# A new order of work in the first four blocks of a conv and squared-ReLU kernel, with one weight half swapped by TensorE

## Chip, cores, metric

One core of one Trainium2 chip. The metric is the device time of one execution in microseconds (us). The mean clock granted to TensorE in one execution lies between 0.995 and 1.000 of full speed. The span of a profile is the same execution as the profiler saw it; it is 1.6 to 2.3 us shorter than the device time.

## The reference, cut to what matters

```python
# 8 sequences of 4096 rows, 192 columns; 8 heads of 24 columns; 7 taps
w = softmax(weight_gen, axis=-1)                   # (8, 4096, 8, 7)
x_unf[b, s, k] = x_pad[b, s + k]                   # 6 rows of zeros ahead
out = einsum('bshk,bskhg->bshg', w, x_unf)         # each row has its own 7 taps
h = maximum(out.reshape(32768, 192) @ w_in, 0)     # w_in 192 x 2048
return (h * h) @ w_out                             # w_out 2048 x 192
```

## The kernel before

All 32768 rows are cut into 64 sub-blocks of 512 and these into blocks: two blocks of one sub-block, then 31 of two. A block goes through four stages, on four engines:

- Softmax (ScalarE exp, VectorE sum, reciprocal, product), in parts of 8 to 32 rows per partition. Part 0 (1024 rows) feeds blocks 0 and 1, part 1 (sub-blocks 2 and 3) block 2, part 2 block 3, part 3 block 4, and so on.
- Weight rows are moved by DMA, multiplied on VectorE into a band matrix (`st_bands`), and TensorE does the convolution as band matmuls (`st_conv`, "C" below). ScalarE copies the result y out of PSUM.
- The first matmul in 8 or 16 units (`st_unit`, "u"): TensorE into one of three PSUM tiles, ScalarE relu into t, VectorE square into g.
- The second matmul in half quarters ("M"): a quarter is 256 rows, summed over all of g into one bank (blocks 0 and 1) or two; then ScalarE copies the bank out, VectorE adds the second bank.

```python
ps_h = ...bufs=3     # three tiles of two banks: h, y of the conv, and before also the spins
ps_o = ...bufs=1     # banks o0 and o1

orders = {0: "uuuuuCuuu", 1: "MuMuuuMuuuMCu", 2: "MuuuuMuuuuMuuuuuuuMCu"}
steady = "MuMuuu" * 3 + "MuuuMCu"
...                                        # softmax and bands: a table by block and unit
at(0, 4, "exp", s1, 0, s1.rh)
at(0, 5, "soft", s1, 0, s1.rh)

spin(42)                                   # matmuls on zeros, to bring TensorE's clock up
band_mask()
s0.load(nc.sync)
load_w_in(w_st[0], 0, nc.sync); x_load_f32(0); load_w_in(w_st[1], 1, nc.sync)
s0.exp(...); s0.total(...); s0.recip(...); s0.scale(...)
nc.scalar.copy(out=w_i[:, 0, 0], in_=w_st[0])
wr_load_sbuf(0, [s0], (0, 2, 1, 4, 3), (nc.sync, nc.gpsimd))   # weight rows of block 0
wr_load_sbuf(1, [s0], range(NT), (nc.gpsimd,))
cross_w_in(0)                              # SBUF to SBUF: halves of 64 partitions exchanged
x_cast(0, nc.scalar.copy)
x_load_f32(1)
nc.scalar.copy(out=w_i[:, 1, 0], in_=w_st[1])
cross_w_in(1)
s1.load(nc.sync)                           # the same queue: softmax weights of part 1
... # bands and conv of block 0, then
nc.gpsimd.memset(x_st[1][:, 0:1], 0.0)     # waits for the cast of x of sub-block 1
for q in range(4): load_w_out(q, 4)
s2.load(nc.gpsimd)
nc.gpsimd.memset(v_big, 0.0)
... # block 0, in it the rows of part 1 moved (also on GpSimd's queue); then
x_load(2); x_load(3)
```

Each half of `w_in` is needed on both halves of the partitions, so it is swapped across them; `cross_w_in` does that with two transfers of 192 KB each.

The softmax here doesn't subtract the row's maximum and nothing guards it: scores larger than these inputs give would overflow.

## Time and profile before

| | before |
|---|---|
| device time, median of 4 | 751.65 us (751.18 to 752.27) |
| span of the profiled run | 749.2 us |
| TensorE / ScalarE / VectorE busy | 739.0 / 623.0 / 621.8 us |
| TensorE idle | 10.2 us |
| first unit of block 0 starts | 15.47 us |
| conv of blocks 2, 3, 4, 5 starts | 36.65, 55.50, 78.41, 100.96 us |

Only the first 100 us are of interest: from there on every block takes 22.5 us with TensorE never idle, but for a few of 22.7 to 23.2. In a timeline line the columns are start, length, engine, line of the program, what was done, how many of them; in brackets the idle time before and what ended it. PE is TensorE, ACT ScalarE, DVE VectorE, POOL GpSimd, SP SyncE. The conv starts are the mile posts of this document: the conv of block n+1 stands at the end of block n.

### The profile page before, as it was taken

The page shows a single profiled execution, that of the slowest core. Times are in us where ns is not written, and L with a number is a line of the kernel's source. Part 1 is how long each engine was busy: PE and PEld are TensorE (multiplying, and loading weights), DVE is VectorE, ACT ScalarE, POOL GpSimd, SP SyncE. Part 2 cuts the span into 40 slices and gives each one's busy share as a digit, 9 for nine tenths or more (in the row PEclk, how much of TensorE's full clock was granted, in tenths as well). Part 3 has the DMA queues.
Part 4 walks back from the last instruction along what each step waited for, and adds up shares of the span by engine and source line. Part 5 has one row for each costly group of instructions (what it writes and reads, how often), then busy time and mean ns, then how long its engine had stood idle before and what let it go on. Part 6 is the DMA issues. An engine that isn't in the chain of part 4 may idle for free.

```text
span 749.2 us, 33282 instructions
## 1 busy us (share of the span) xinstructions
PE 739.0 (99%) x15106; PEld 559.8 (75%) x15106; DVE 621.8 (83%) x1001; ACT 623.0 (83%) x753; POOL 87.9 (12%) x127
## 2 busy tenths in 40 slices
PE   8899999999999999999999999999999999999998
PEld 4658777777887777777877777777778777777787
DVE  5889998998789888887888888898888987677853
ACT  4898888888888888888888888888888888888883
POOL 3522220001101000011000110001100011001000
PEclk9999999999999999999999999999999999999999
DMA  8846444446453344543245442365441354441312
GB/s 231 129 74 135 79 68 109 101 78 138 93 109 69 74 77 80 131 86 65 46 80 139 86 80 49 55 138 108 59 79 47 57 109 80 59 75 50 50 45 65
DMA packets 122329, 65.20 MB, mean 87 GB/s; under 512 B 83881, under 2 KB 118668, under 8 KB 121676
## 3 DMA queue, kind: packets, MB, share of 16 engines
q1 hardware_dynamic: 77868, 46.05, 22.4%
q0 software_dynamic: 44176, 16.93, 20.6%
q8 instruction: 118, 1.93, 1.1%
q14 instruction: 23, 0.19, 0.1%
q10 hardware_dynamic: 144, 0.10, 0.0%
HBM read 48.61 MB, written 28.70 MB: 103 GB/s over the span
## 4 chain that ended last, share of the span: by engine, by line
PE 88%; DVE 5%; DMA 3%; ACT 1%; issue 1%; SPq 0%; POOL 0%; DVEq 0%; ACTq 0%
PE o L453 42%; PE h L419 40%; PE yp L394 6%; DVE g L431 2%; DVE bd L326 1%; DMA xt<-in_x_dram 1%; ACT t L428 1%; DMA x_st<-in_x_dram 1%; DMA vd<-v_big 1%; DVE v_first L217 1%; DVE ssum L202 0%; DVE rcp L209 0%; DMA wg<-in_weight_gen_dram 0%; DVE o_sb L469 0%; POOL wr L308 0%
## 5 line engine op out<-in xcount | busy, mean ns | idle before, releaser
L428 ACT ACTIVATE t<-h 128x1024 f16<-128x1024 f32 x512 | 497.1, 1027 | 66.9 <-PE h L419 66.6
L431 DVE TENSOR_TENSOR g<-t 128x1024 f16<-128x1024 f16 x512 | 334.5, 687 | 101.9 <-ACT t L428 99.1
L453 PEld LDWEIGHTS <-g 64*128 64x128 f16 (+1 forms) x8032 | 353.0, 94 | 55.7 <-issue 5.0
L453 PE MATMUL o<-w_o,g 64*128 64x192 f16 (+1 forms) x8032 | 386.1, 243 | 1.7 <-DMA w_o<-in_moe_w_out_dram 0.7
L419 PE MATMUL h<-y,w_i 64*128 64x512 f16 (+1 forms) x3168 | 379.8, 370 | 2.1 <-ACT t L428 0.9
L419 PEld LDWEIGHTS <-w_i 64*128 64x128 f16 x3168 | 165.5, 94 | 114.7 <-issue 5.0
L326 DVE TENSOR_TENSOR bd<-wr,mask 128x4160 f16<-128x4160 f16 (+3 forms) x89 | 149.4, 1702 | 4.6 <-DMA wr<-v_first 4.6
L278 POOL DMA_DIRECT2D xt<-in_x_dram x62 | 51.3, 832 | 446.1 <-PE yp L394 422.8
L467 ACT COPY o_sb<-o 128x384 f32<-128x384 f32 x129 | 62.3, 483 | 33.2 <-PE o L453 33.2
L469 DVE TENSOR_TENSOR o_sb<-o,o_sb 128x384 f32<-128x384 f32 x123 | 68.2, 554 | 8.0 <-ACT o_sb L467 5.6
L405 ACT CAST y<-yp 128x1024 f16<-128x1024 f32 (+1 forms) x64 | 48.2, 803 | 16.5 <-PE yp L394 16.5
L394 PE MATMUL yp<-bd,xt 128*32 128x104 f16 (+8 forms) x3864 | 52.0, 208 | 1.8 <-DMA xt<-in_x_dram 1.2
L394 PEld LDWEIGHTS <-xt 128*32 128x32 f16 (+3 forms) x3864 | 46.1, 91 | 8.0 <-issue 6.4
L217 DVE TENSOR_TENSOR v_big<-ex,rcp 128x112 f16<-128x112 f32 (+1 forms) x136 | 27.3, 263 | 1.8 <-DMA vd<-v_big 0.6
L195 ACT ACTIVATE ex<-wg 128x448 f32<-128x448 f32 (+2 forms) x44 | 27.2, 618 | 1.9 <-DMA wg<-in_weight_gen_dram 1.9
L202 DVE TENSOR_REDUCE ssum<-ex 128x64 f32<-128x448 f32 (+2 forms) x44 | 26.1, 593 | 2.4 <-ACT ex L195 2.4
L209 DVE RECIPROCAL rcp<-ssum 128x64 f32<-128x64 f32 (+2 forms) x44 | 23.7, 539 | 1.5
L268 POOL DMA_DIRECT2D xt<-in_x_dram x7 | 3.8, 547 | 136.9 <-PE yp L394 136.9
L308 POOL DMA_DIRECT2D wr<-v_first x31 | 16.8, 562 | 15.4 <-DVE v_first L217 15.3
L516 PE MATMUL wp<-warm 128*128 128x512 f16 x42 | 11.1, 432 | 1.3 <-DVE warm L508 1.3
L516 PEld LDWEIGHTS <-warm 128*128 128x128 f16 x42 | 4.5, 109 | 7.4 <-issue 2.5
L217 DVE TENSOR_TENSOR v_first<-ex,rcp 128x112 f16<-128x112 f32 (+1 forms) x48 | 9.1, 255 | 0.3
(19 smaller groups left out, 24.5 us busy)
## 6 DMA issues: line engine op xcount, KB each, us to landing
out_dram<-o_sb SPq DMA_DIRECT2D x63, 384.0 KB, 2.9
xt<-in_x_dram POOLq DMA_DIRECT2D x42, 240.0 KB, 6.0
wg<-in_weight_gen_dram SPq DMA_DIRECT2D x4, 1064.0 KB, 7.7
xt<-in_x_dram POOLq DMA_DIRECT2D x20, 192.0 KB, 5.6
wr<-vd SPq DMA_DIRECT2D x38, 80.0 KB, 5.0
vd<-v_big SPq DMA_DIRECT2D x5, 512.0 KB, 5.5
wg<-in_weight_gen_dram SPq DMA_DIRECT2D x5, 392.0 KB, 4.2
wg<-in_weight_gen_dram SPq DMA_DIRECT2D x3, 616.0 KB, 5.5
```

What stands on the lines that cost most here:

```text
L195: nc.scalar.activation(out=self.ex[:, lo:hi].rearrange("p r g k e -> p (r g) k e"), in_=self.wg[:, lo:hi].rearrange("p r (g e) k -> p (r g ...
L217: eng.tensor_tensor(out=bass.AP(tensor=v.tensor, offset=v.offset + lo * H * SL + lo % SL * 2 + g * SL * 2, ap=[list(v.ap[0]), [H * SL + 2, ...
L278: eng.dma_start(out=dst[:, first:last], in_=ap)
L326: nc.vector.tensor_tensor(out=bd_t[j][:, H * lo : H * (lo + len(tiles) * n)].rearrange("p (g m c) -> p g m c", g=shape[1], c=2 * SL), in0= ...
L394: nc.tensor.matmul(out=yps[k // per][p0 : p0 + m, col + a : col + b], lhsT=x_t[s][:, i, 32 * q : 32 * q + m], rhs=bd[:, h // 2, h % 2, a - ...
L405: nc.scalar.copy(out=y[:, k0:k1, 0:th], in_=yp[:, 0 : (k1 - k0) * th].rearrange("p (k c) -> p k c", c=th),)
L419: nc.tensor.matmul(out=h[:, half, jj * th : (jj + 1) * th], lhsT=w_in_chunk(u * per + jj, slot, half), rhs=y_t[j][r0 : r0 + RT, k, 0:th], ...
L428: nc.scalar.activation(out=t1, in_=h, func=ActF.Relu)
L431: nc.vector.tensor_tensor(out=g, in0=t1, in1=t1, op=AluOp.mult)
L453: nc.tensor.matmul(out=oo[:, cc * Dm : (cc + 1) * Dm], lhsT=g[r0 : r0 + n, cc * P : (cc + 1) * P], rhs=w_o[r0 : r0 + n, fc, :], start=(fc ...
L467: nc.scalar.copy(out=o_sb, in_=o[0][:, c])
L469: nc.vector.tensor_tensor(out=o_sb, in0=o[1][:, c], in1=o_sb, op=AluOp.add)
```

## The change

Its intent: the first four blocks get an order written out step by step, in which units, half quarters, exps (E), softmax (S), bands (B) and loads of softmax weights (L) stand where their inputs are ready; X is the cast of x. The number behind E, S or L is the part, that behind B or X the sub-block. Ten units run before the first half quarter, the softmax of part 1 comes earlier, x and `w_out` are fetched earlier. Blocks 0 and 1 use the two banks of the second matmul in turn. The first half of `w_in` is swapped by three matmuls with a permutation matrix; the spins are split around them.

```diff
+    def half_swap():                       # swap[p, m] = 1 where |p - m| = 64
...
+    def cross_w_in_by_pe(q):
+        n = NQ + NQ // 2
+        for a in range(0, n, 2 * TB):
+            b = min(a + 2 * TB, n)
+            pt = ps_h.tile([P, 2 * TB], f32, name="pt", tag="h")
+            for c in range(a, b, TB):
+                nc.tensor.matmul(out=pt[:, c - a : c - a + TB], lhsT=swap, rhs=w_i[:, q, 0, c : c + TB], ...)
+            nc.scalar.copy(out=w_i[:, q, 1, a:b], in_=pt[:, 0 : b - a])
...
-        spin(42)
-        band_mask()
+        spin(25)
+        half_swap()
+        band_mask()
+        nc.gpsimd.memset(v_big, 0.0)
...
-        cross_w_in(0)
         x_cast(0, nc.scalar.copy)
+        cross_w_in_by_pe(0)
+        spin(14)
...
-        nc.gpsimd.memset(x_st[1][:, 0:1], 0.0)
+        nc.gpsimd.tensor_copy(out=gate, in_=x_st[1][:, 0:1])
         for q in range(4):
             load_w_out(q, 4)
         s2.load(nc.gpsimd)
-        nc.gpsimd.memset(v_big, 0.0)
-        orders = {0: "uuuuuCuuu", 1: "MuMuuuMuuuMCu", 2: "MuuuuMuuuuMuuuuuuuMCu"}
+        x_load(2)                          # x_load(3) follows behind conv 1
+        plans = {
+            0: "B1 X1 u u u E1 S1 u C u u u u",
+            1: "L3 u u B2 M E2 B3 u M E2 u u S2 u M u C u S2 M",
+            2: "L4 u u u E3 M u u u M B4 u u u u M B5 S3 u u u u M u E3 C u",
+            3: "L5 L6 M S3 u u u M u u u u M u M B6 E4 u u u M M B7 u u S4 u E4 M u C M u",
+        }
...
-                        o = new_o(ps_o, 1 if j < 3 else 2)
+                    o = new_o(ps_o, 1, qt % 2) if j < 2 else new_o(ps_o)
```

From block 4 on each engine has the order it had.

## The prediction

> **What bounds the kernel now.** I read the page first (busy shares and the 40 slices), then the waits of all engines, then TensorE's and ScalarE's timelines for the first 125 us, then a table of stretches cut at the starts of the conv groups, because one conv starts each block.
>
> ```profile
> PE 739.0 (99%) x15106; PEld 559.8 (75%) x15106; DVE 621.8 (83%) x1001; ACT 623.0 (83%) x753; POOL 87.9 (12%) x127
> ...
> PE   8899999999999999999999999999999999999998
> ```
>
> TensorE is busy in 739.0 of 749.2 us, so idle time is 10.2 us, 1.4%. The slices show where: the first two and the last. No new order can gain 2% out of that.
>
> ```profile
> core 0: us, PE busy (x) PEld busy (x) DVE busy (x) ACT busy (x) POOL busy (x), PEclk, DMA share, GB/s
> 12.29:35.37 23.08, 19.70 (x389) 15.84 (x389) 19.74 (x32) 17.90 (x22) 11.25 (x16) 1.00 0.89 168
> 35.37:55.50 20.13, 18.80 (x286) 11.34 (x286) 17.76 (x32) 17.46 (x23) 4.91 (x8) 1.00 0.43 75
> 55.50:78.41 22.91, 22.77 (x475) 18.54 (x474) 21.19 (x38) 20.01 (x25) 4.95 (x8) 1.00 0.54 111
> 78.41:100.96 22.55, 22.55 (x475) 16.61 (x473) 21.77 (x43) 20.03 (x26) 4.73 (x8) 1.00 0.37 67
> 100.96:123.49 22.53, 22.53 (x475) 16.55 (x473) 21.80 (x42) 19.63 (x25) 4.95 (x8) 1.00 0.48 101
> ```
>
> The last two rows are the steady block: 22.5 us, TensorE never idle. The first two rows hold 4.7 us of idle TensorE while neither ScalarE nor VectorE is full. The reader should see that the loss is a matter of who waits when, not of too much work. The waits themselves, from TensorE's and ScalarE's timelines (start, length, engine, line, what; in brackets the idle time before and what ended it):
>
> ```profile
> 20.16 0.83 PE L419 MATMUL h<-y,w_i 64*128 64x256 f16 x12
> 21.89 1.52 PE L419 MATMUL h<-y,w_i 64*128 64x256 f16 x24 [0.90 <-ACT t L428]
> 24.14 1.48 PE L453 MATMUL o<-w_o,g 128*128 128x192 f16 x16 [0.72 <-DMA w_o<-in_moe_w_out_dram]
> ...
> 26.42 1.02 ACT L428 ACTIVATE t<-h 128x1024 f16<-128x1024 f32 x1 [1.13 <-PE h L419]
> 28.23 0.48 ACT L467 COPY o_sb<-o 128x384 f32<-128x384 f32 x1 [0.78 <-PE o L453]
> ...
> 36.65 1.58 PE L394 MATMUL yp<-bd,xt 128*32 128x104 f16 x118 [1.05 <-DMA xt<-in_x_dram]
> ```
>
> Units that follow each other run at ScalarE's pace (a relu starts every 0.92 us: four take 3.77), not at TensorE's 0.69. Then the second matmul arrives in one lump (21.9 to 36.7 us) and ScalarE starves; then the conv of block 2 waits for x.
>
> **What the Trainium skill says.** "Perfetto Trace Analysis", section "Optimization Strategy", says that a kernel may have several regimes with different contended engines, and that interleaving the regimes can help. The trace agrees: relu-bound until 24 us, DMA-bound at 35 to 37, TensorE-bound from 64. The same page, "Matmuls", advises that independent groups rotate through PSUM banks so that one's evacuation overlaps the next; blocks 0 and 1 here use one bank for every group. The trace shows little loss from it, since the copy of 0.48 us at 28.23 is done long before the next group at 30.19. "TensorE: Matmul & The Clock Gate", Part 1, says that the array runs at half clock until about 3.4 us of activity: the first spins here stand 0.43 us apart, those after 5.07 us 0.21, so it agrees. "DMA: Bandwidth & Descriptors", "Anatomy of one DMA", puts about 2 us of fixed cost on each transfer; here a move of weight rows takes 1.7 to 3.7 us to land (median 2.4), which is why a softmax must end some 3.4 us before its band can start (25.82 to 29.23).
>
> **The change part by part.** Prices from TensorE's timeline, start to start: unit of 512 columns 0.65 (57.01 to 57.66), unit of 256 columns 0.69, half of a second-matmul quarter (M) 1.43 on one bank and 1.32 on two, conv of a double block 1.51, of a single one 0.88. Work against time, stage by stage:
>
> conv 1 to conv 2: 0.88 + 10 x 0.69 + 4 x 1.43 = 13.5, took 16.09: 2.6 lost.
> conv 2 to conv 3: 1.51 + 0.69 + 15 x 0.65 + 4 x 1.43 = 17.7, took 20.13: 2.4 lost.
> conv 3 to conv 4: 1.51 + 16 x 0.65 + 8 x 1.32 = 22.5, took 22.91: 0.4 lost.
>
> So at most 5.4 us are to be had behind the first conv of block 1. The instructions of each engine are the same in kind and number, but for those of the swap; all is moved.
>
> *Start and swap.* 42 spins become 25 + 14 plus 3 swap matmuls. 25 spins end near 5.07 + 15 x 0.21 = 8.3; the swap waits for the cast of w_in, done at 8.71, takes 3 x 0.21, and 14 spins end near 12.3, as 42 did. ScalarE takes two copies more, estimated from the 0.80 us copy of 768 columns at 1.0 + 0.6 = 1.6 us; they fit into its idle stretch from 9.61 to 11.22. Two transfers of 192 KB go, which lets the second x load be issued 1.2 us earlier. But the first unit at 15.47 hangs on another chain: weights land, exp, three VectorE steps until 8.35, rows moved by 11.49, five bands until 14.09, conv, copy at 14.62. None of it is touched. Gain at the first unit: 0. GpSimd's earlier fills (swap, mask, v_big 2.5 us) end near 8, by estimate, just ahead of the moves it issues at 8.65.
>
> *Blocks 0 and 1.* I stepped the new order by hand with those cadences: relu 0.92, exp 0.82 (784), 0.51, 0.43; VectorE square 0.60, softmax 3.26 for 784 columns, 1.95 and 1.65 for the smaller pieces, bands 2.24 per sub-block; three PSUM buffers, freed 1.05 us after a relu begins. The softmax of part 1 comes after three units instead of five; its exp at 19.3 (its load, issued at 14.39 and 5.2 us to landing, allows 19.6 at worst), VectorE done with it at 23.5 instead of 25.8. Ten units instead of eight run ahead of the first M: that costs some relu-bound time (first M at 25.3), but both of its halves find their squares ready, where the second one took 1.88 before. x of sub-block 2 is fetched some 6 us earlier, and that of sub-block 3 lands near 32.5 (issued near 27, 4.7 to 6.4 us). Bands 2 and 3 end at 32.5. Conv 2 starts near 33.1; the first unit of block 2 starts at 36.8. Before, it started at 40.35 with one M (1.43) more done: gain 40.35 - 1.43 - 36.8 = 2.1.
>
> *Block 2.* Its M come singly between three or four units instead of bunched early, so ScalarE, which has some 18 us of work there (16 relus at 0.92, two copies of y at 1.38 together, two exps, two to three copies at 0.45) against 17.7 of TensorE's, never starves. Conv 3 near 52.3 instead of 55.50, equal work done: gain 3.2.
>
> *Block 3.* VectorE no longer has to run seven squares and two softmax pieces ahead of the second M (62.89, 1.86 us against 1.48). Conv 4 near 73.4 with one M still owed: 73.4 + 1.32 = 74.7 against 78.41: gain 3.7.
>
> *Two banks in turn.* No wait on the single bank shows, so about 0 by itself; it is what allows an M directly behind another.
>
> From block 4 on every engine has the order it had. Sum: 3.7 us by steps that assume nothing collides. I take off 0.5 for what hand steps miss: 3.2.
>
> **The rivals.** (1) The gain is hidden: ScalarE bounds blocks 0 to 2 whatever the order. For it: in 35 to 56 us ScalarE is busy 17.46 of 20.13. Against: it idles 2.7 there and 5.2 of 23.08 in the stretch before. Then the gain is 1 to 1.5, at 750.5. (2) A transfer takes the place of the waits removed: x of sub-block 3 or the rows of part 1 come late, as DMA engines are 0.89 busy until 35 us and the loads of w_out now overlap the load of softmax weights. Each us late at conv 2 costs one us; time 749.5 to 751. (3) The start gets faster because the swap unloads the DMA queues: rows land sooner, conv 0 starts sooner. For it: bands waited 3.15 us for them. Against: the moves are issued ahead of the swap transfers. It would add 0.5 to 1: 747.7. (4) VectorE becomes the bound in blocks 2 and 3, where it is busy 21.19 of 22.91; the gain stops at 2: 749.9.
>
> **Range and chances.** The measured time is 2.7 above the span; I take the gain off the time: 751.88 - 3.2 = 748.7. The floor is the full 5.4 with rival 3, about 746; the bad end is rivals 1 and 2, about 750.6. Executions of before lie within 0.8 us. Range 747.0 to 750.6. Two per cent would be 15 us, more than all idle time: chance of faster 0.01, within 2% 0.985, slower 0.005.
>
> **What would show it.** Right: idle of TensorE falls from 10.2 to about 7; first unit still at 15.4 to 15.5; conv 2 near 33, conv 3 near 52.3, conv 4 near 73.4; no wait for x at conv 2; steady blocks of 22.5 unchanged, so the end shifts by what conv 4 gained. Wrong: a wait of conv 2 or its bands on a DMA; relu stretches in 26 to 34 with long idle; M slower than 1.43 in block 3, which would mean squares late; or later blocks longer, giving the gain back.

## The result, and the profile after

The changed kernel took 748.50 us (median of 4, 747.71 to 750.48) against 751.65. The ratio was 0.9961 (95% interval 0.9941 to 0.9982). A ratio here and below is the mean time of the one kernel's runs over the mean of the other's of the same rounds, so not quite the ratio of the medians. In five more rounds, on chip A of the experiments: 748.41 against 751.02, ratio 0.9965 (0.9950 to 0.9980). The predicted 748.7 was 0.2 off.

The page's busy line and its slices of TensorE, of the changed kernel:

```profile
PE 739.0 (99%) x15106; PEld 556.5 (75%) x15106; DVE 621.8 (83%) x1001; ACT 624.7 (84%) x755; POOL 88.8 (12%) x130
...
PE   8999999999999999999999999999999999999998
```

TensorE's busy time is the same 739.0 us to the tenth. The span went from 749.2 to 746.6, so all of the gain is idle time: 10.2 became 7.6. The second slice went from 8 to 9.

The stretches of the changed kernel from conv to conv (busy time of each engine, granted clock, DMA share, GB/s), to be set against the five rows in the prediction:

```profile
core 0: us, PE busy (x) PEld busy (x) DVE busy (x) ACT busy (x) POOL busy (x), PEclk, DMA share, GB/s
13.04:33.13 20.09, 17.75 (x373) 14.72 (x372) 18.79 (x31) 16.63 (x20) 8.96 (x14) 1.00 0.92 167
33.13:52.77 19.64, 19.64 (x304) 12.26 (x303) 18.22 (x32) 18.30 (x22) 4.91 (x8) 1.00 0.42 76
52.77:73.99 21.22, 21.22 (x442) 15.23 (x441) 19.75 (x35) 19.25 (x25) 4.92 (x8) 1.00 0.52 120
73.99:98.79 24.80, 24.18 (x507) 20.72 (x505) 23.25 (x45) 21.03 (x27) 4.75 (x8) 1.00 0.35 61
98.79:121.34 22.55, 22.55 (x474) 16.62 (x472) 21.82 (x42) 19.62 (x25) 4.93 (x8) 1.00 0.47 101
```

Blocks 2 and 3 now have no idle TensorE at all. But the fourth row is longer than a steady block: 24.80. It holds one half quarter more than before (1.32), which makes 22.5 + 1.32 = 23.8; about 0.95 is left over, 0.62 of it marked idle. At conv 4 the changed kernel was 78.41 - 73.99 - 1.32 = 3.1 us ahead, at conv 5 it is 100.96 - 98.79 = 2.2 ahead. So a part of the gain was given back.

At conv 5 both kernels have done the same work, so 2.2 us is what these two traces show of the gain. The measured 2.6 and 3.15 are more, and the mean granted clock for every execution of the rounds below says where to look for a part of that. In the rounds on chip A, five of the eleven executions of before had a mean clock of 0.997 or 0.998 and took 752.0 us on average; the six at 0.999 or above took 750.4. Of the changed kernel one of six was at 0.998 (750.45); the five at 1.000 took 748.3. Near full clock the difference is thus 2.1 us, as in the traces, out of 2.5 between the means of all; the rest goes with before losing clock more often. On chip C this split does not show (below).

The waits by name of TensorE, of the changed kernel:

```profile
PE wp L539 <- DVE warm L531: 1.3, 1, 1.3
PE h L441 <- ACT t L450: 0.9, 1, 0.9
PE h L441 <- ACT y L427: 0.9, 1, 0.9
PE o L475 <- DVE o_sb L491: 0.6, 1, 0.6
PE yp L416 <- DVE bd L348: 0.2, 1, 0.2
```

The waits for x (1.2) and for `w_out` (0.7) are gone. Last but one stands what did not exist before: a matmul into o that waits 0.6 for VectorE to empty a bank. It shows in the timeline of TensorE after conv 4, and in that of VectorE:

```profile
75.52 1.49 PE L475 MATMUL o<-w_o,g 64*128 64x192 f16 x32
76.85 0.81 PE L441 MATMUL h<-y,w_i 64*128 64x512 f16 x6
77.57 0.24 PE L475 MATMUL o<-w_o,g 64*128 64x192 f16 x1
78.43 1.48 PE L475 MATMUL o<-w_o,g 64*128 64x192 f16 x31 [0.62 <-DVE o_sb L491]
```

```profile
75.87 0.83 DVE L239 TENSOR_TENSOR v_first<-ex,rcp 128x112 f16<-128x112 f32 x4
76.62 1.28 DVE L453 TENSOR_TENSOR g<-t 128x1024 f16<-128x1024 f16 x2
77.83 0.55 DVE L491 TENSOR_TENSOR o_sb<-o,o_sb 128x384 f32<-128x384 f32 x1
```

The last half quarter of block 2 (75.52) ends at 77.0, and ScalarE copies its first bank out from 77.04 to 77.52. The sum that empties the second bank starts at 77.83 on VectorE, behind a softmax piece and two squares. The next quarter begins one unit later, at 77.57; its first matmul finds its bank free, the second does not.

### The profile page after: what moved, and what is told of

Its sections match the earlier page's. It is cut to its first block, busy times and chain, and to the rows that moved or that the text cites. A ratio compares the mean times of both kernels' runs of the same rounds, so it can differ in the third digit from the quotient of the medians.

```text
span 746.6 us, 33289 instructions
## 1 busy us (share of the span) xinstructions
PE 739.0 (99%) x15106; PEld 556.5 (75%) x15106; DVE 621.8 (83%) x1001; ACT 624.7 (84%) x755; POOL 88.8 (12%) x130
## 4 chain that ended last, share of the span: by engine, by line
PE 94%; DVE 2%; issue 1%; DMA 1%; ACT 1%; POOL 0%; DVEq 0%; ACTq 0%
PE o L475 45%; PE h L441 43%; PE yp L416 6%; DVE g L453 1%; DVE bd L348 1%; DMA wr<-v_first 0%; DMA wg<-in_weight_gen_dram 0%; POOL wr L330 0%; ACT t L450 0%; DVE v_first L239 0%; ACT ex L217 0%; DVE ssum L224 0%; DVE rcp L231 0%; DVE o_sb L491 0%; ACT y L427 0%
## 5 line engine op out<-in xcount | busy, mean ns | idle before, releaser
L441 PEld LDWEIGHTS <-w_i 64*128 64x128 f16 x3168 | 162.6, 94 | 117.2 <-issue 5.2
```

The lines of the kernel that those rows point to most:

```text
L441: nc.tensor.matmul(out=h[:, half, jj * th : (jj + 1) * th], lhsT=w_in_chunk(u * per + jj, slot, half), rhs=y_t[j][r0 : r0 + RT, k, 0:th], ...
```

## The experiments

The executions of one kernel scatter by 0.8 to 3.6 us, as much as is at stake, so each experiment was read in two ways: by timed rounds against before, and by its trace. The trace needs one correction. The first unit started at 15.35 to 16.91 us in 14 traces, as its input transfers came. So the column "conv 5 - u1" measures from the first unit. b_ is before with an edit, a_ the changed kernel with an edit. Chips: A for the first four, B for the next four, C for the last four; before and the changed kernel in the first two rows were profiled elsewhere.

| kernel | median us | ratio to before | first unit | conv 2 | conv 5 | conv 5 - u1 |
|---|---|---|---|---|---|---|
| before | 751.65 | 1 | 15.47 | 36.65 | 100.96 | 85.49 |
| changed | 748.50 | 0.9961 | 15.55 | 33.13 | 98.79 | 83.24 |
| after_again (A) | 748.41 | 0.9965 | 16.01 | 33.60 | 99.27 | 83.26 |
| b_loads (A) | 751.81 | 1.0007 | 16.91 | 37.99 | 102.28 | 85.37 |
| a_late_x (A) | 748.98 | 0.9972 | 15.46 | 33.44 | 99.10 | 83.64 |
| a_late_soft (A) | 749.90 | 0.9985 | 15.35 | 34.36 | 100.31 | 84.96 |
| a_no_swap (B) | 750.16 | 0.9987 | 16.55 | 35.51 | 101.24 | 84.69 |
| a_one_bank (B) | 748.19 | 0.9960 | 16.38 | 33.97 | 99.64 | 83.26 |
| a_old_3 (B) | 747.29 | 0.9954 | 15.93 | 33.51 | 98.24 | 82.31 |
| a_m_before_c (B) | 748.15 | 0.9962 | 15.72 | 33.31 | 98.99 | 83.27 |
| b_spin47 (C) | 751.54 | 0.9993 | 15.51 | 37.17 | 101.65 | 86.14 |
| b_loads47 (C) | 750.69 | 0.9992 | 16.55 | 36.20 | 100.52 | 83.97 |
| a_no_swap47 (C) | 750.17 | 0.9979 | 16.62 | 36.09 | 101.75 | 85.13 |
| a_s4_late (C) | 748.45 | 0.9954 | 15.69 | 33.27 | 98.94 | 83.25 |

Each interval of a ratio is about 0.0013 to either side, 1 us; differences between kernels of one chip are told by their medians, with their ranges where these lie apart. "Conv 2" is where the bulk of the group starts (in before its first two matmuls ran at 35.37, then waited); in the changed order one half quarter (1.43) stands behind it that before had done. At conv 5 all have done the same. All twelve gave the right result.

### The same kernel again

> The changed kernel once more, for a tighter interval and to see whether its trace repeats. All theories: 2.6 us under before (ratio 0.9965), conv groups of blocks 2, 3, 4 and 5 at 33.1, 52.8, 74.0 and 98.8 us within 0.1.

Ratio 0.9965; conv starts at 33.60, 53.24, 74.50, 99.27. All are late by 0.5, as is the first unit; from the first unit on the trace repeats to 0.05 us. That is why the last column is fit for comparing, and why a single trace's absolute times are not.

### Only the new order of loads

```diff
 # before, with
+        nc.gpsimd.memset(v_big, 0.0)                    # behind band_mask()
-        nc.gpsimd.memset(x_st[1][:, 0:1], 0.0)
+        nc.gpsimd.tensor_copy(out=gate, in_=x_st[1][:, 0:1])
-        nc.gpsimd.memset(v_big, 0.0)
+        x_load(2)                                       # behind s2.load; x_load(3) behind conv 1
```

> The kernel before with only the new order of loads: w_out and x of sub-block 2 fetched before the moves of part 1, v_big cleared at the start. Theory 'order' (the units, softmax and second matmul in a new order make most of the gain): the waits for w_out (0.7) and for x (1.2) go, but the squares for the second M and ScalarE's pace then bind, so it gains 1.0 to 1.4 us of the 2.6; conv 2 near 35.2. Rival 'loads' (the transfers were all of it): gains 2.3 or more.

Ratio 1.0007: no gain at all, which neither theory had said. Its trace shows why it could not answer the question. It is shown on a_no_swap (below), which has the same fault and also 42 spins in one piece: stretches of 5 us, the granted clock third from the end:

```profile
10.00:15.00 5.00, 3.47 (x60) 1.71 (x59) 2.65 (x6) 2.22 (x2) 2.42 (x5) 0.99 0.77 175
15.00:20.00 5.00, 4.11 (x56) 3.37 (x57) 3.57 (x4) 2.49 (x3) 2.53 (x5) 0.50 0.85 220
20.00:25.00 5.00, 4.95 (x126) 3.79 (x123) 3.82 (x8) 4.74 (x7) 2.17 (x4) 0.83 1.47 226
```

TensorE ran at half its clock from about 15 to 21.7 us. In b_loads the same stretch 15 to 20 has 0.50. The 42 spins end at 12.0 to 12.2; in these two traces the bands came late (12.69 and 12.35 against 11.49 in before), TensorE had little to do for some 3 us (in a_no_swap it was busy 0.15, 0.64 and 0.68 of the three us from 12 to 15), and then the granted clock fell. It is no single case: four of the six executions of b_loads have a mean clock of 0.995 to 0.998. It was tried again with more spins, below.

### x as late as before

```diff
         s2.load(nc.gpsimd)
-        x_load(2)
...
                     if j == 0:
+                        x_load(2)
                         x_load(3)
```

> The changed kernel with x of sub-block 2 fetched where before fetched it, after block 0 and the moves of part 1. Theory 'order': the moves start 2 us earlier than in before, so the fetch is issued near 26.5 instead of 28.8 and lands near 34.3; conv 2 slips from 33.1 to about 34.3, and 1.0 to 1.3 us of the 2.6 are lost. Rival 'loads': conv 2 falls back to about 36.6 and all is lost. Rival 'hidden transfer' (ScalarE is the bound, slack takes up the delay): under 0.4 lost at conv 3.

Median 748.98 against 748.41 of after_again, 0.6 more; the trace says 0.4 (83.64 against 83.26):

```profile
33.44 1.58 PE L416 MATMUL yp<-bd,xt 128*32 128x104 f16 x118 [0.16 <-DMA xt<-in_x_dram]
```

The conv of block 2 does wait for x again, but only 0.2 to 0.4 us. The expectation of 1.0 to 1.3 was too high because x landed at 33.4, not 34.3. The early fetch matters little once the softmax of part 1 is early, since the rows of that part stand ahead of x in GpSimd's queue. "Hidden transfer" set the bound nearest: its under 0.4 is about what the trace shows. But no slack took the delay up, as it had said: the 0.4 is there at conv 3 and still at conv 5. "Loads" is refuted for x; the earlier fetch of `w_out` was not taken back in any run.

### The softmax of part 1 as late as before

```diff
-            0: "B1 X1 u u u E1 S1 u C u u u u",
+            0: "B1 X1 u u u u E1 u C S1 u u u",
```

> The changed kernel with the softmax of part 1 where before had it: exp after four units instead of three, VectorE's part after five instead of three. Theory 'order': VectorE is done with it near 25.7 instead of 23.5, bands 2 and 3 end about 2 us later (34.3 instead of 32.4) and the second M waits for squares; conv 2 at 34.2 to 34.8, 0.9 to 1.5 us of the gain lost at the end. Rival 'loads': less than 0.3 lost, since x and w_out come as early as in the changed kernel.

1.5 us of the gain lost by the medians (749.90 against 748.41), 1.7 by the trace. TensorE and VectorE:

```profile
34.36 1.87 PE L416 MATMUL yp<-bd,xt 128*32 128x104 f16 x118 [1.19 <-DVE bd L348]
```

```profile
30.18 4.59 DVE L348 TENSOR_TENSOR bd<-wr,mask 128x4160 f16<-128x4160 f16 x3 [1.47 <-DMA wr<-v_first]
```

The softmax ends at 25.7, the moves let the bands start at 30.2 instead of 27.8, and the conv waits for them. The theory is confirmed in the chain of softmax, moves, bands, conv. Not confirmed is its side effect: the second half quarter did not wait for squares (1.49 us, as long as all).

### Without the swap on TensorE

```diff
-        spin(25)
-        half_swap()
+        spin(42)
...
+        cross_w_in(0)
         x_cast(0, nc.scalar.copy)
-        cross_w_in_by_pe(0)
-        spin(14)
```

> The changed kernel with the first half of w_in swapped by two transfers again and 42 spins. Theory 'order': the first unit starts at 15.5 either way, because rows, bands and conv 0 set it; the x of sub-block 1 is issued 1.2 us later, which delays the gate and the loads of w_out and x by as much, still early enough; end within 0.3 us of the changed kernel. Rival 'start' (the swap unloads the queues and is worth 0.5 to 1): slower by 0.5 to 1.

750.16 us (749.30 to 751.34) against 748.19 (747.37 to 748.70) of a_one_bank on the same chip, whose trace is the changed kernel's: 2.0 us slower. My theory fails here. Its trace has the half clock shown above, which left open whether it is the transfers or the earlier end of the spins. The clock is not all of it: four of the six executions ran at 1.000 and took 749.74 on average, still 1.6 above the mean of a_one_bank (748.12, all at 0.999 or 1.000).

### One bank

```diff
-                    o = new_o(ps_o, 1, qt % 2) if j < 2 else new_o(ps_o)
+                    o = new_o(ps_o, 1) if j < 2 else new_o(ps_o)
```

> The changed kernel with the second matmul of blocks 0 and 1 always on bank o0, as before. In the changed kernel no quarter of these blocks starts within 2 us of the copy of the one before, so theory 'order' expects no wait and the same end within 0.2 us. Rival 'banks' (the turn of banks makes the order possible): a wait of 0.5 us or more at some quarter and 0.5 to 1 us lost.

83.26 against 83.24, no wait on o before block 4. The banks in turn are worth nothing in this order.

### Block 3 in the old order

```diff
-  3: "L5 L6 M S3 u u u M u u u u M u M B6 E4 u u u M M B7 u u S4 u E4 M u C M u",
+  3: "M S3 L5 L6 u M u u u M u M B6 u u u M E4 u M B7 u u u M E4 u u u M C S4 u",
```

> The changed kernel with block 3 in the old order (its last half quarter before conv 4 again). Theory: block 3's new order gains little where softmax of part 3 has one piece done in block 2; the old order puts two halves ahead of three units, so the second half finds its squares late (about 0.4 lost by conv 4), but the wait of 0.6 to 0.9 us for the bank at 77.6 to 78.4 goes, so the end is 0.4 to 0.6 us earlier than the changed kernel. Rival (the new block 3 is worth the 0.5 us that the steps by hand gave it, and the wait at 78 is no loss): 0.5 us later.

The best kernel by the median, and better than either theory had said: 747.29 us (746.65 to 748.86), by the median 0.9 under a_one_bank and a_m_before_c on the same chip (the ranges overlap), and 0.95 less in the trace (82.31). The ratios (0.9954 against 0.9960 and 0.9962, each within 0.0016) do not tell them apart; the trace does. Its stretches from conv 3 to conv 5:

```profile
53.15:75.69 22.54, 22.54 (x475) 16.56 (x473) 20.93 (x37) 20.24 (x26) 4.92 (x8) 1.00 0.51 113
75.69:98.24 22.55, 22.55 (x475) 16.61 (x473) 21.80 (x43) 20.03 (x26) 4.75 (x8) 1.00 0.37 67
```

Both are steady. So the old order of block 3 loses nothing by conv 4 (I had expected 0.4), since 22.54 is what the new order took as well (21.22 + 1.32). And the 0.95 that was given back after conv 4 is not.

### Only the last half quarter of block 3 ahead of the conv

```diff
-  "... B7 u u S4 u E4 M u C M u"
+  "... B7 u u S4 u E4 M u M C u"
```

> The changed kernel with only the last half quarter of block 3 moved to before conv 4. In the changed kernel that half ends at 76.85, its second copy waits on VectorE behind a softmax piece until 78.4, and TensorE waits 0.6 us for the bank. Theory (the wait is a loss of the new order, given back after conv 4): the wait goes, conv 5 comes at 97.8 to 98.1 instead of 98.8 and the end is 0.6 to 0.9 us earlier. Rival (conv 4's copy of y then stands in the open instead, as TensorE has one unit less to do behind it): no gain.

No gain: 83.27, and the wait is still there, at the same matmul, because the sum is still late on VectorE:

```profile
78.63 1.48 PE L475 MATMUL o<-w_o,g 64*128 64x192 f16 x31 [0.70 <-DVE o_sb L491]
```

```profile
78.03 0.55 DVE L491 TENSOR_TENSOR o_sb<-o,o_sb 128x384 f32<-128x384 f32 x1
```

The half quarter now ends at 75.6 and ScalarE's copy at 76.1, and still the sum starts at 78.03. The softmax piece (74.84 to 76.9) and two squares that it stands behind did not move.

### 47 spins in before

```diff
-        spin(42)
+        spin(47)
```

> The kernel before with 47 spins instead of 42, nothing else. Theory 'clock' (in part of the executions of before the spins end near 12.1 us, the bands come late, TensorE idles too long and block 0 runs at half clock, as the traces of the two kernels with 42 spins in one piece showed from 15 to 22 us): the granted clock is 1.00 throughout, the median falls by 0.3 to 1.0 us and the spread of 3.8 us narrows. Theory 'order alone': the same as before within 0.3.

751.54 (750.86 to 751.82) against 751.83 for before on the chip (749.57 to 752.80): the median fell by 0.3, the ratio's interval reaches from 0.9981 to 1.0006, the spread was smaller. Too little to confirm "clock". And the granted clock was not 1.00 throughout: it fell to 0.50 at about 22 us, after a wait that the profile of before does not have. TensorE, then ScalarE:

```profile
21.02 0.71 PE L419 MATMUL h<-y,w_i 64*128 64x256 f16 x9 [1.62 <-DMA w_i<-w_i]
```

```profile
22.06 0.94 ACT L195 ACTIVATE ex<-wg 128x784 f32<-128x784 f32 x1 [1.91 <-DMA wg<-in_weight_gen_dram]
```

The fifth unit waited for the second half of the swapped `w_in`, and the exp of part 1 for its weights. Both transfers stand behind the first swap in the same queue. In the profile of before that exp had run without a wait:

```profile
19.97 0.96 ACT L195 ACTIVATE ex<-wg 128x784 f32<-128x784 f32 x1
```

Its load, issued at 14.4 in both, landed after 5.2 us there and after 7.6 here. What that and the lost clock cost in time is not clear: this execution (clock 0.998) was the fastest of its five, and the three at 1.000 took 751.5 to 751.8.

### The loads alone, with 47 spins

The edit, on b_loads:

```diff
-        spin(42)
+        spin(47)
```

> The kernel before with the new order of loads and 47 spins. Without the half clock that spoilt the first try: theory 'order' as written there, 1.0 to 1.4 us under before with 47 spins, conv 2 some 19.7 us behind the first unit (21.2 in before, 17.6 in the changed kernel). Rival 'loads': 2 us or more. If it is again no faster, the loads gain nothing by themselves.

The clock stayed at 1.00 in this trace. Behind the first unit the loads gain 85.49 - 83.97 = 1.5, conv 2 comes 19.65 behind it as expected. But the first unit itself came 1.1 later than in the profile of before. The time fell by 0.9 against b_spin47 by the medians (750.69 against 751.54), and not at all by the ratios (0.9992 against 0.9993). What the loads gain in time is left open; it is not 2 us.

### Without the swap, with 47 spins

The edit, on a_no_swap:

```diff
-        spin(42)
+        spin(47)
```

> The changed kernel without the swap on TensorE, but with 47 spins. Theory 'clock' (what the swap is worth is that its wait moves the spins' end from 12.1 to 13.0 to 13.5 us): granted clock 1.00, time as the changed kernel within 0.4 us. Rival 'swap' (the two transfers themselves delay rows and bands): 1 us or more slower than the changed kernel, at full clock, with the first unit near 16.5.

750.17 (750.03 to 751.12), as slow as with 42 spins (750.16, on chip B), and 1.7 above a_s4_late of the same chip (748.06 to 748.86). Four of the five executions ran at 0.999 or 1.000 and took 750.03 to 750.26. So it is the swap and not the place of the spins: theory "clock" falls, and "swap" stands.

How the swap costs its time is less sure, because the profiled execution is the fifth and slowest: 751.12 us, clock 0.998. The first unit came at 16.62. Then, in the timelines of ScalarE and of TensorE, and last ScalarE's line of the changed kernel:

```profile
21.28 0.93 ACT L217 ACTIVATE ex<-wg 128x784 f32<-128x784 f32 x1 [0.93 <-DMA wg<-in_weight_gen_dram]
```

```profile
23.17 4.03 PE L441 MATMUL h<-y,w_i 64*128 64x256 f16 x40 [1.71 <-ACT t L450]
```

```profile
19.14 0.95 ACT L217 ACTIVATE ex<-wg 128x784 f32<-128x784 f32 x1
```

The exp of part 1 waits for its weights until 21.28; in the eight traces with the swap on TensorE it ran between 19.08 and 19.98. Since it stands ahead of the relus in ScalarE's queue, TensorE waits 1.7 us for a PSUM tile (23.17), and everything behind it slips. With that wait the granted clock fell here too (third from the end), to 0.50 until 27 us:

```profile
22.00:23.00 1.00, 0.00 (x0) 0.00 (x0) 0.76 (x1) 1.00 (x2) 0.46 (x1) 1.00 1.48 166
23.00:24.00 1.00, 0.83 (x12) 0.80 (x13) 0.97 (x2) 1.00 (x3) 0.00 (x0) 0.80 1.53 169
```

The load of the exp's weights is the last big one of the start on SyncE's queue. With the swap by DMA it is issued at 14.8 instead of 14.0, and 384 KB more are under way ahead of it. The later issue alone is not it: in a_one_bank that load was issued at 14.8 as well, and the exp ran at 19.98 without a wait. The other transfers of the queue were slower too: the two pieces of x of sub-block 1 took 3.4 and 5.5 us to landing here against 2.6 (the one on record) in the changed kernel, the second swap 4.5 against 2.9. But of the six traces with the swap by DMA only this one and b_spin47 have the exp wait for its weights, so this chain is one way in which the swap costs time, not shown to be all of the 1.7.

Not settled is why the first unit was late (16.55 to 16.91) in all four kernels that clear v_big early and swap by DMA. In them the first cast of `w_in` started at 8.13 to 8.38, in the eight with the swap by TensorE at 7.03 to 8.16, in the two that clear v_big late at 7.05 and 7.24. That load comes before any swap, so the two transfers cannot be its cause. The earlier clearing by GpSimd (3.70 instead of 4.56) goes with it, but no run changed that alone.

### The softmax piece of part 4 behind the last half quarter

```diff
-  "... B7 u u S4 u E4 M u C M u"
+  "... B7 u u u E4 M u C M S4 u"
```

> The changed kernel with only the first softmax piece of part 4 moved in block 3: from before the last three units to behind the last half quarter. Theory 'VectorE's order' (the sum of the last quarter stands behind 2 us of softmax on VectorE, so the bank comes free late; moving the half quarter did not help because it did not move the softmax): no wait for the bank near 78, conv 4 to conv 5 takes 23.9 us instead of 24.8, the end 0.6 to 0.9 us earlier than the changed kernel, near 747.4. Rival (the wait comes from something else in the new block 3, for instance two halves in a row): no change.

Conv 4 to conv 5 took 24.59 instead of 24.80. The wait got shorter, 0.35, and did not go. TensorE, then VectorE:

```profile
78.51 1.48 PE L475 MATMUL o<-w_o,g 64*128 64x192 f16 x31 [0.35 <-DVE o_sb L491]
```

```profile
77.90 0.56 DVE L491 TENSOR_TENSOR o_sb<-o,o_sb 128x384 f32<-128x384 f32 x1 [1.62 <-ACT o_sb L489]
```

VectorE now stands ready and waits for ScalarE's copy, which has to come first; the copy starts as the half quarter ends (77.39) and is done at 77.87. Behind the conv only one unit (0.65) lies between this half quarter and the next quarter; copy and sum (0.48 + 0.55) do not fit into it. So my theory gave half the cause. The wait seems to have two: the softmax piece ahead of the sum, and the last half quarter behind the conv. Moving either alone gains 0 to 0.2 of this stretch (at conv 5 nothing, 83.25, since 0.2 had been lost in block 2); a_old_3, which has neither, gains 0.95. As a_old_3 changes all of block 3, no run shows the two moves together and nothing else.

## Why the prediction was right, point by point

- **The total.** Predicted 748.7, measured 748.5 and 748.4. That it is this close is luck in part. The steps gave 3.7 us by conv 4, the traces 3.1; the 0.5 held back for what hand steps miss covers that. Another 0.95, then lost in block 4, was in no step, so the traces show 2.2 in place of 3.2. The measured 3.15 and 2.6, each uncertain by 1 us or more, are larger than the traces by scatter and by before's lower clock, which the prediction did not count on. The 2.7 us that it puts between time and span sets the median (751.88) against the span of another execution; the profiled one took 751.43.
- **The milestones.** First unit 15.47 foretold, 15.55 seen; conv 2 33.1 and 33.13; conv 3 52.3 and 52.77; conv 4 73.4 and 73.99. That fits its prices for relu, square and bands. The spins were mis-timed: the first 25 ended near 9.3, not 8.3, and the last at 13.1, not 12.3, without harm, as the conv then still waited 0.17 for a band. (That the first spins of before run at half rate is seen in their spacing only; the granted clock of the views says 1.00 there.)
- **Blocks 0 and 1.** The step "softmax of part 1 earlier, so bands 2 and 3 are ready for conv 2" was right and is shown: undone, it costs 1.5 us. The waits for `w_out` and x went as foretold.
- **The step that failed: the swap.** The text gave it "0", because the chain to the first unit is not touched. That chain was the wrong place to look. Chip C gives the parts with equal spins and in the same rounds: 751.54 for b_spin47, 750.17 with the new order and loads but the swap by DMA, 748.45 with the swap by TensorE too (a_s4_late). So about 1.4 us are the order with its loads (the ranges of these two overlap a little), and 1.7 the swap (of it at most 0.2 for the moved softmax piece). The exp at 19.3, from which the steps by hand went on, was met with the swap on TensorE (19.08 to 19.98 in eight traces, never waiting). With the swap by DMA its weights came too late in two of six traces (22.06 in b_spin47, 21.28 in a_no_swap47), a risk that the profile of before, at 19.97, did not show. Whether that is where the 1.7 us go stays open: the first unit was late too in a_no_swap and a_no_swap47 (16.55 and 16.62), and why is not settled. What the swap would be worth in the old order was not run.
- **Rival 3** came nearest to this in cause (the queues are unloaded), yet put it on the rows of block 0 and on 0.5 to 1 us. The rows were not sooner: the bands began at 11.57, in before at 11.49.
- **The banks in turn**: about 0 foretold, 0 measured.
- **Block 3.** The last 0.5 of the steps (3.2 to 3.7) was put down to block 3's new order; block 3 took a steady 22.54 in either order. What helps there may be that part 3 has one softmax piece done in block 2; no run took that back.
- **"The end shifts by what conv 4 gained"** was wrong. The last 0.95 was given back at 77.6 to 78.4. I had foreseen later blocks growing longer only as a general risk; the sum that empties the bank was in no step.
- **The chance of 0.985 for "within 2%"** rested on the 10.2 us of idle time and held.

## What to carry to other kernels

A transfer that is not on the chain you follow can still delay what is queued behind it. Before pricing the removal of one at zero, look for the next load of the same queue that an in-order engine will wait for. When an order is written out by hand, every engine that has to empty a PSUM bank belongs in the steps, with its own queue; here one softmax piece and one conv between the wrong neighbours gave back a third of the gain. And one profile shows one start: the same exp ran freely in one trace of the old kernel and waited 1.9 us in another that differs by five spins. So read a second profile before building on the first 20 us, and look at the granted clock of every timed execution, and at whether the profiled one is typical, before explaining a difference of 1 or 2 us.

## What the Trainium skill lacked or had wrong

- "TensorE: Matmul & The Clock Gate", Part 1, has the array fall back to half clock after at least one idle window of about 3.4 us. Here the granted clock fell to 0.50 at about 14.9 us without any such gap: in a_no_swap the longest idle stretches ahead of it were 0.85 and twice 0.28 us, between small conv matmuls, TensorE being busy 0.15, 0.64 and 0.68 of the three us before. In b_spin47 and a_no_swap47 it fell after gaps of 1.62 and 1.71 us. In the changed kernel, with 0.83, 0.62 and 0.45 from 13 to 16 us, and in before, with 0.64, 0.55 and 0.53, it did not fall. The page's passage on a second failure mode, with short idle stretches between groups of matmuls, fits better, but neither says how little activity is too little.
- "Perfetto Trace Analysis", "Matmuls", advises to rotate groups through PSUM banks. It does not say that the gain hangs on where the emptying instructions stand in their engines' queues: turning the banks was worth 0.0 us here, and a quarter that came one unit too early waited 0.35 to 0.70 us.
- I found no page that says how far the time to landing of loads varies from execution to execution: the first unit started between 15.35 and 16.91 us in 14 traces of one input set, and the same load of softmax weights (392 KB) landed after 5.2 us, so that its exp could start at 19.97, or after 7.6, so that it waited until 22.06, in two kernels that differ by five spins.
